# The first sweep's side work dealt at 0.6 instead of 0.56 in an attention, FFT and feed-forward kernel

## Chip, cores, metric

The kernel runs on one core of one Trainium2 chip. The metric is the device time of one execution in microseconds (us), lower is better; a time without further words is the median of several executions.

## What is computed

The inputs are q, k and v of shape (8 batches, 12 heads, 448 tokens, 64), two gains, and two weight matrices of 768 x 3072 and 3072 x 768, all fp32.

```python
q_n, k_n = rmsnorm(q, g_q), rmsnorm(k, g_k)
attn = softmax(q_n @ k_n.T / 8)
x = (attn @ v), heads side by side           # (8, 448, 768)
u = x + real(fft(fft(x, axis=1), axis=2))
un = (u - mean(u)) / sqrt(var(u) + 1e-6)     # over the last axis
out = u + relu(un @ w_ch1) @ w_ch2
```

## The kernel before, in words

Every batch goes through two kinds of work. The **side work** of a batch, `aux(b)` (L771), is attention over six pairs of heads, then three *folds* (L594, sums and differences of the attention result that only VectorE makes) and the two transforms (`spectral`, L644: `y` matmuls, `ab` matmuls, then four token tiles with the `x` transposes). The **feed-forward** of a batch, `ffn(b)` (L1035), is one *sweep* over 60 pieces of weights: 24 `up(m)` of 18 matmuls each (L1054) and 36 `down(g, d)` of 12 each (L1075), in the order up 0, then six groups of four ups (three in the last) and six downs. Each fp32 product is made from rounded high and low halves, hence three passes.

The sweep of batch b is interleaved with the side work of batch b + 1. Both are Python generators that yield a planned cost at each step: an up 3420, a down 2280; in the side work 420 for each transposed half of q or k, 760 for each of four rows of a pair's softmax, 420 + 6 x 1180 + 760 for the values of a pair of batch 1, 2000, 2000 and 3000 for its three folds, 1080 for each of four `y` steps, 980 for each of two `ab` steps and 620 for each of four token tiles. `merge` (L1106) takes a piece of the feed-forward, then side steps until the side's cost has reached the feed-forward's cost times a ratio. The ratio is `RATIO_FIRST` for batch 0 (L1160) and `RATIO` = 0.49 for the others.

Ahead of the first sweep, batch 0's side work runs alone, with 22 steps of batch 1's (`AHEAD`, L45) mixed in: these carry batch 1 through the values of its first pair. What the first sweep is given is the rest: pairs 1 to 5, folds, transforms.

The first sweep also converts weights. `bits_of` (L784) loads fp64 weights into one of two wide buffers (`dbl`) and makes fp32 of them on ScalarE (L798, L799), VectorE (L800, L804, L808) and GpSimd (L812); `convert` (L815) splits the value into high and low halves (L817 on ScalarE, L818 on VectorE). Of the 60 pieces 14 are converted before (`convert_some`, L908): downs 2 and 3 of groups 0 to 4 and ups 3, 7, 11 and 15. A piece is taken from a stream of three buffers, two streams by turns, so a piece's successor by six is refilled when it is taken. Later sweeps load converted pieces.

The order in which each engine works is not the order of the Python calls alone: the program is laid out ahead of the run by a planner (`schedule_with_timeline_sim`, L1180), which takes instructions in the order of the calls as far as its own estimate has them ready, and puts later ones ahead of those that it thinks are waiting. On the chip each engine then follows that fixed order. Result tiles of `ffn` take turns in two banks; ScalarE's relu `hs` (L1061) and VectorE's `hs` (L1062) or `acc` (L1091) free them.

Of the kernel before, what the change touches and what calls it, by code (L numbers as in the profile page):

```python
# [37 lines left out]


RATIO = 0.49  # L40
RATIO_FIRST = 0.56
CONVERT_EARLY = 0.12
EARLY = 2
DFT_STEP = 40
# [48 lines left out]
def spectral_block(ctx, tc, q, k, v, g_q, g_k, w1, w2, d1, d2, out, nb=B):  # L93
# [677 lines left out]
    def aux(b):  # L771

        EO, uns[b] = [], {}
        yield from attention(b, EO)
        yield from spectral(b, xTs[b], EO, uns[b])
# [371 lines left out]
    def behind_first():  # L1147

        fences.update(turned)
        for n, x in enumerate(second):  # L1150
            fences.clear()
            yield x
            if n < SIDE_BEHIND:
                fences.update(turned)

    for b in range(nb):
        merge(
            ffn(b, ffn_input(b, uns.pop(b)) if b else first),
            behind_first() if b == 0 else aux(b + 1) if b + 1 < nb else iter(()),
            RATIO if b else RATIO_FIRST,  # L1160
        )
# [24 lines left out]
```

## Time and profile before

| | us |
|---|---|
| median of 3 runs | 2147.34 (2145.43 to 2149.45) |
| profiled execution, its own time | 2143.77 |
| its span, first to last instruction | 2142.0 |
| first up of the first sweep starts at | 182.8 |
| first up of the second sweep starts at | 458.1 |

The profile is of one execution. TensorE (PE) is busy 97% of the span, VectorE (DVE) 72%, ScalarE (ACT) 48%, GpSimd (POOL) 16%. These shares mean little for the first 460 us, which differ from the rest; the rows below are therefore taken stretch by stretch. Times in the rows are counted from the first instruction.

### The profile page before, as it was taken

The numbers are of one execution on the slowest core, as the hardware profiler recorded it, in microseconds if no ns is written. First come the engines' busy times: TensorE is split into PE (matmuls) and PEld (weight loads), VectorE is DVE, ScalarE is ACT, GpSimd is POOL, SyncE is SP. The second block draws the span as 40 slices with busy tenths as digits, with TensorE's granted clock in tenths as the row PEclk, the third lists the DMA queues.
The fourth block names the chain that finished last, engine by engine and source line by source line (L and its number), as shares of the span: only waits on it lengthen the run. The fifth ranks groups of instructions, "written<-read, shape, count | busy, mean of one in ns | idle before, by whom it ended". The sixth has DMA issues, their size and how long they took to land.

```text
span 2142.0 us, 31168 instructions
## 1 busy us (share of the span) xinstructions
PE 2074.2 (97%) x11256; PEld 1846.0 (86%) x11256; DVE 1550.9 (72%) x2948; ACT 1024.4 (48%) x2182; POOL 342.5 (16%) x182
## 2 busy tenths in 40 slices
PE   7877999899999999999999999999999999999998
PEld 4555878799999999999999999999999989999998
DVE  6888889977885878757886778858787578764122
ACT  6857875456542555345552465425553455422100
POOL 3324334311110111001110111101010011000000
PEclk8988999999999999999999999999999999999999
DMA  6538867776556855657555755667556674458774
GB/s 186 183 122 287 267 230 239 265 243 194 175 166 197 236 169 170 188 184 225 162 176 176 237 182 173 180 188 233 168 174 186 193 210 138 152 174 250 236 251 150
DMA packets 283550, 423.86 MB, mean 198 GB/s; under 512 B 181075, under 2 KB 200516, under 8 KB 283396
## 3 DMA queue, kind: packets, MB, share of 16 engines
q1 hardware_dynamic: 278962, 419.75, 63.6%
q10 hardware_dynamic: 4434, 2.11, 0.4%
q8 instruction: 90, 1.47, 0.3%
q14 instruction: 64, 0.52, 0.1%
HBM read 362.01 MB, written 65.31 MB: 199 GB/s over the span
## 4 chain that ended last, share of the span: by engine, by line
PE 84%; DVE 5%; DMA 4%; ACT 4%; POOL 1%; issue 1%; SPq 0%; DVEq 0%; ACTq 0%; POOLq 0%
PE o L1075 30%; PE h L1054 29%; PE S L416 6%; PE av L529 4%; PE pt L517 4%; DMA dbl<-w 2%; PE y L660 2%; PE qk L352 1%; PE av L491 1%; ACT P L117 1%; PE S L411 1%; PE oT L1011 1%; PE x L691 1%; PE un L923 1%; POOL mag L812 1%
## 5 line engine op out<-in xcount | busy, mean ns | idle before, releaser
L1075 PE MATMUL o<-hs,w 128*128 128x448 f32 x3456 | 787.0, 371 | 6.2 <-ACT hs L117 2.5
L1054 PE MATMUL h<-unT,w 128*128 128x448 f32 x3456 | 788.6, 370 | 0.4 <-ACT unT L117 0.4
L1075 PEld LDWEIGHTS o<-hs,w 128*128 128x128 f32 x3456 | 636.4, 188 | 61.1 <-ACT hs L117 2.8
L1054 PEld LDWEIGHTS h<-unT,w 128*128 128x128 f32 x3456 | 637.5, 188 | 53.8 <-issue 1.9
L117 ACT ACTIVATE P<-S,mn 112x448 f32<-112x448 f32 x384 | 244.1, 638 | 231.4 <-DVE mn L117 227.0
L117 DVE TENSOR_REDUCE mn<-S 112x1 f32<-112x448 f32 x384 | 233.2, 617 | 45.0 <-PE S L416 36.3
L117 ACT ACTIVATE hs<-h 128x448 fp32r<-128x448 f32 x192 | 104.4, 544 | 297.0 <-PE h L1054 296.2
L117 DVE TENSOR_TENSOR acc<-o,acc 128x448 f32<-128x448 f32 (+1 forms) x240 | 147.0, 615 | 122.4 <-PE o L1075 121.0
L117 DVE SCALAR_TENSOR_TENSOR hs<-h,hs 128x448 fp32r<-128x448 f32 x192 | 119.1, 620 | 138.8 <-ACT hs L117 137.6
L117 POOL TENSOR_TENSOR qkn<-raw 112x1024 f32<-112x1024 f32 x36 | 68.2, 1894 | 687.4 <-PE qk L352 590.1
L117 POOL TENSOR_TENSOR ss<-ss,nhalf 112x16 f32<-112x16 f32 x48 | 144.0, 3001 | 200.4 <-DVE ss L117 172.9
L117 ACT CAST T<-pt 128x448 fp32r<-128x448 f32 x216 | 113.5, 532 | 108.4 <-PE pt L517 105.9
L529 PE MATMUL av<-T,vhl 128*128 128x448 f32 x432 | 151.7, 383 | 0.0
L117 DVE TENSOR_TENSOR T<-pt,T 128x448 fp32r<-128x448 f32 x216 | 131.6, 616 | 25.8 <-ACT T L117 24.7
L416 PE MATMUL S<-KD,QT 128*112 128x448 f32 x328 | 126.7, 386 | 4.8 <-ACT P L117 4.4
L117 DVE TENSOR_SCALAR P<-P,sm 112x448 f32<-112x448 f32 x288 | 126.8, 479 | 4.0 <-DMA values<-v 0.3
L517 PE MATMUL pt<-ident,P 112*128 112x112 f32 x864 | 125.2, 259 | 0.0
L416 PE MATMUL S<-rounded,QT 128*112 128x448 f32 x328 | 120.3, 367 | 0.1
L517 PEld LDWEIGHTS pt<-ident,P 112*128 112x128 f32 x864 | 103.7, 140 | 16.3 <-DVE R L117 0.3
L812 POOL TENSOR_TENSOR mag<-mag,dbl 128x768 uint32<-128x768 uint32 (+1 forms) x33 | 77.4, 2347 | 153.9 <-DVE mag L808 99.1
L117 POOL TENSOR_TENSOR rstd<-st,nhalf 112x1 f32<-112x1 f32 (+2 forms) x32 | 19.2, 600 | 494.0 <-DVE st L117 487.9
L529 PEld LDWEIGHTS av<-T,vhl 128*128 128x128 f32 x432 | 80.8, 188 | 8.3
(120 smaller groups left out, 2502.0 us busy)
## 6 DMA issues: line engine op xcount, KB each, us to landing
w<-w SPq DMA_DIRECT2D x192, 768.0 KB, 4.8
w<-w SPq DMA_DIRECT2D x288, 512.0 KB, 4.2
dbl<-w SPq DMA_DIRECT2D x20, 768.0 KB, 5.4
dbl<-w SPq DMA_DIRECT2D x13, 1024.0 KB, 5.6
raw<-q SPq DMA_DIRECT2D x96, 112.0 KB, 3.4
raw<-k SPq DMA_DIRECT2D x96, 112.0 KB, 3.9
values<-v SPq DMA_DIRECT2D x96, 96.0 KB, 4.4
u_dram<-u SPq DMA_DIRECT2D x24, 336.0 KB, 7.5
```

What stands on the lines that cost most here:

```text
L117: ins = emit(*args, **kwargs)
L352: nc.tensor.transpose(pt[:, c * C : (c + 1) * C], qk[:, i, c].rearrange("t h d -> t (h d)"), ident[:C, :C],)
L411: nc.tensor.matmul(s_, QT[hs, x, cs], KD[hs, z], start=step == 0, stop=step == 2)
L416: ins = nc.tensor.matmul(s_, QT[:, h, cs], K[:, h], start=step == 0, stop=step == 1)
L491: nc.tensor.matmul(av[:, :S], vhl[:, 3 * h + j].rearrange("s h d -> s (h d)"), T, start=h + j == 0, stop=False,)
L517: nc.tensor.transpose(pt[:, c * C : (c + 1) * C], Pc[c][:, 512 * h + j * 128 : 512 * h + (j + 1) * 128], ident[:C, :C],)
L529: nc.tensor.matmul(av[:, :S], lv, T[:, i], start=(j == 0 and i == 0), stop=False)
L660: nc.tensor.matmul(o, src[:, par, t0 : t0 + n], D1[:, ri, par, cols], start=i != 1, stop=i != 0,)
L691: nc.tensor.transpose(xp[:n, i * 128 : (i + 1) * 128], src[:, 3 * half + i], ident)
L812: behind(nc.gpsimd.tensor_tensor(out=bits, in0=bits, in1=low, op=ALU.add))
L1054: pace(nc.tensor.matmul(o, w[:, a, c], unT[c][:, z], start=n == 0, stop=n == 17))
L1075: pace(nc.tensor.matmul(o, w[:, a, f], hs[4 * g + f][:, z], start=n == 0, stop=n == 11))
```

## The change

One constant is different. Nothing is added or removed from what any engine does; the places of the side steps between the pieces of the first sweep are what the constant sets.

```diff
 RATIO = 0.49
-RATIO_FIRST = 0.56
+RATIO_FIRST = 0.6
 CONVERT_EARLY = 0.12
```

## Rows read from the trace of the kernel before

**Rows 1.** Busy time in stretches: us, each engine's busy us (instructions), clock, DMA share, GB/s.
```profile
core 0: us, PE busy (x) PEld busy (x) DVE busy (x) ACT busy (x) POOL busy (x), PEclk, DMA share, GB/s
183.00:320.00 137.00, 132.00 (x664) 110.79 (x665) 113.90 (x170) 104.58 (x199) 49.05 (x26) 0.98 0.77 255
320.00:380.00 60.00, 58.32 (x296) 48.65 (x295) 56.44 (x77) 34.47 (x65) 28.28 (x11) 1.00 0.70 233
380.00:420.00 40.00, 34.55 (x179) 30.49 (x178) 38.41 (x49) 19.10 (x30) 12.44 (x6) 0.91 0.77 266
420.00:458.00 38.00, 38.00 (x210) 35.01 (x210) 32.05 (x67) 20.92 (x40) 7.46 (x6) 1.00 0.77 267
458.00:707.00 249.00, 248.81 (x1389) 227.71 (x1388) 186.37 (x376) 115.83 (x256) 30.95 (x16) 1.00 0.63 190
```
**Rows 2.** Timeline of PE around 400 us: start, length, what, idle time before and releaser.
```profile
400.02 0.47 PE L1075 MATMUL o<-hs,w 128*128 128x448 f32 x1 [2.46 <-ACT hs L117]
401.58 1.11 PE L1075 MATMUL o<-hs,w 128*128 128x448 f32 x2 [1.10 <-DVE hs L117]
404.59 3.61 PE L660 MATMUL y<-D,eo 128*113 128x130 f32 x16 [1.89 <-DVE eo L117]
```
**Rows 3.** Timeline of ACT in the same stretch.
```profile
393.33 0.19 ACT L117 COPY xT<-xT 128x1 f32<-128x1 f32 x1 [4.51 <-DVE xT L117]
395.26 0.89 ACT L798 ACTIVATE mag<-dbl 128x768 f32<-128x768 f32 x1 [1.75 <-DMA dbl<-w]
...
398.63 0.90 ACT L798 ACTIVATE mag<-dbl 128x768 f32<-128x768 f32 x1 [1.66 <-DMA dbl<-w]
399.44 0.52 ACT L117 ACTIVATE hs<-h 128x448 fp32r<-128x448 f32 x1
```
**Rows 4.** Timeline of DVE (last fold, conversions) and of POOL in the same stretch.
```profile
384.50 0.68 DVE L818 TENSOR_TENSOR w<-mag,w 128x512 fp32r<-128x512 f32 x1
...
388.56 2.67 DVE L804 TENSOR_SCALAR mag<-mag 128x768 uint32<-128x768 uint32 x1
...
393.74 1.52 DVE L117 TENSOR_TENSOR eo<-xT 128x449 f32<-128x449 f32 x2
...
397.74 0.55 DVE L804 TENSOR_SCALAR mag<-mag 128x768 uint32<-128x768 uint32 x1
...
405.46 1.08 DVE L117 TENSOR_TENSOR tot<-tot,eo 128x900 f32<-128x900 f32 x1
...
388.29 2.52 POOL L812 TENSOR_TENSOR mag<-mag,dbl 128x1024 uint32<-128x1024 uint32 x1 [6.79 <-DMA values<-v]
```
**Rows 5.** Timeline of PE: last value matmul of batch 1's pairs 1, 2, 3 and 5.
```profile
255.47 0.91 PE L498 MATMUL av<-R,values 128*128 128x448 f32 x2
281.70 0.92 PE L498 MATMUL av<-R,values 128*128 128x448 f32 x2
316.41 0.91 PE L498 MATMUL av<-R,values 128*128 128x448 f32 x2
...
383.43 0.91 PE L498 MATMUL av<-R,values 128*128 128x448 f32 x2
```
**Rows 6.** Timeline of PE: one whole up and one whole down.
```profile
426.46 3.84 PE L1054 MATMUL h<-unT,w 128*128 128x448 f32 x18
...
445.36 2.69 PE L1075 MATMUL o<-hs,w 128*128 128x448 f32 x12
```
**Rows 7.** Busy time in three stretches of the early sweep, columns as in rows 1.
```profile
200.00:220.00 20.00, 17.00 (x82) 14.46 (x81) 16.29 (x25) 14.20 (x27) 5.66 (x4) 0.91 0.82 251
220.00:260.00 40.00, 38.62 (x198) 32.58 (x197) 35.32 (x52) 32.20 (x63) 18.69 (x8) 1.00 0.89 288
280.00:320.00 40.00, 39.57 (x200) 32.05 (x199) 30.73 (x50) 29.48 (x58) 13.36 (x9) 1.00 0.75 250
```
**Rows 8.** Waits of PE in 183 to 458 us: total, times, longest; then one DVE group there.
```profile
PE S L416 <- ACT P L117: 4.4, 4, 2.0
...
L818 DVE TENSOR_TENSOR w<-mag,w 128x512 fp32r<-128x512 f32 x26 | 26.5, 1018 | 0.4 <-ACT w L817 0.4
```

## The prediction

> **What bounds the kernel now.** I read the busy times by stretch first [rows 1]. From 458 us on the kernel is TensorE alone: 248.81 of 249 us busy at full clock. An edit that only re-places side steps of the first sweep can gain nothing there, and can lose only if it makes that flow wait. In the first sweep PE is idle for 5.0 us of 183 to 320, 1.7 of 320 to 380, 5.45 of 380 to 420, and not at all after. The granted clock says the rest: 0.91 over 380 to 420 means 18% of 40 us at the lower of the two levels, 7.2 us in which half the work is done, so 3.6 us lost; likewise 0.98 of 137 us is 2.7 us. So the sweep holds 12.2 us of idle time and 6.3 us of clock, 18.5 in all, and 9.0 of them (5.45 + 3.6) stand in one place, 380 to 420. That is all that a better deal could win, and the largest single prize in it is 9.0.
>
> Next what PE waits for in that place [rows 2]: 2.46 us for ScalarE's `hs`, 1.10 for VectorE's `hs`, 1.89 for the `eo` of the last fold, which the first `y` matmul needs. Together 5.45, the whole idle time of the stretch. Why `hs` is late is seen on ACT [rows 3]: it stands in ACT's order behind a copy that waited 4.51 us for VectorE and two conversion steps that waited 1.75 and 1.66 us for weights. VectorE is what stands behind this: 56.44 of 60 us busy in 320 to 380, 38.41 of 40 in 380 to 420 [rows 1], while in 280 to 320 it had 9.3 of 40 us free [rows 7]. The last fold took from 393.74 to 406.5 on VectorE [rows 4], with steps of conversions between its own, as the one at 397.74. So the reading is: VectorE is overfull in the last half of the sweep's side work and has room just before.
>
> **What the change moves.** It removes and adds no instruction and no wait of its own, so every cost is one of place. The planned costs say where. The side work left is 4620 (eleven halves of q or k at 420) + 15200 (five pairs' softmax) + 41300 (five pairs' values at 8260) + 7000 (folds) + 8760 (transforms) = 76,880; the sweep is 24 x 3420 + 36 x 2280 = 164,160. At 0.56 the last side step is dealt when the sweep has reached 76,880 / 0.56 = 137,286, which is behind down(4,4) at 137,940; at 0.6 at 128,133, behind down(4,0) at 128,820. The end of the side work moves four downs forward. Counting the same way: the last value step of pairs 1 to 5 moves from down(0,4), down(1,1), up 12, up 14, up 17 to down(0,3), down(1,0), up 11, up 13, down(3,3); the folds from up 15, down(3,3), up 18 to up 13, down(3,0), down(3,4); the `y` steps from up 19 and 20 and down(4,0) to ups 17 and 18. In time, a piece is 3.84 us for an up and 2.69 for a down [rows 6]. The last fold passes down(3,5), up 17 and up 18: 2.69 + 3.84 + 3.84 = 10.4 us of feed-forward that now comes behind it. The tail passes four downs, 10.8 us.
>
> Does the chip follow the deal? The last value matmul of a pair tells its place [rows 5]. Against the deal at 0.56 pair 1 comes five pieces late (dealt at down(0,4), run just ahead of down(1,0)), pair 2 three late, pair 3 two, and pair 5 on its place, at the end of up 17. From pair 1 to 2 it took 26.2 us, from 2 to 3 34.7, and 67.0 for the two pairs behind. So early on the side work is held by its own chain (it ran a pair in 26.2 us when it was behind), and the ratio hardly matters; from pair 3 on it has caught up and the deal holds it back. There 0.6 acts: I take pair 5 to end some 7 to 9 us sooner, with the three pieces that it passes run later.
>
> **The sum.** Work taken off 320 to 400 has to fit before: 280 to 320 has 9.3 us of VectorE free [rows 7], so the moved steps find room there. Whatever passes behind the folds takes its conversions along, so fewer of them stand between the fold's operations. The `y` wait (1.89) is the one that the change reaches directly; the clock loss (3.6) follows the idle time. The two `hs` waits (3.56 together) come from ACT's order behind conversions and may stay. Bounds: from below 9.0 (all of it goes), from above 0 (the same queues form one group sooner) or a loss (a second such place). I take 1.89 + 3.6 = 5.5 us gained, because the hs waits alone, 3.56 in two pieces, lie near those of 1.7 us in 60 that left the clock at 1.00 in 320 to 380 [rows 1]; they are also not far from the 3.0 of 200 to 220, with clock 0.91 [rows 7], so the gain is not safe. At the end of the sweep nothing is gained: 420 to 458 has no idle time to win, and what follows is as full [rows 1].
>
> The profiled execution took 2143.77 us, 1.77 around its span of 2142.0; the median is 3.57 above it. I put the difference on the median: 2147.34 - 5.5 = 2141.8 (2138.3 by the profiled execution).
>
> **The rivals.** *The queues move along* (0.30). VectorE is overfull from 320 on whatever the order. If the fold is merely overfull sooner, the stall of 9.0 us stands one group earlier at the same price: 2147, give or take 3. For it: the lag of rows 5, and that the planner's order, not the deal alone, sets the place. Against it: the 9.3 us free in 280 to 320. The change not doing what it says is this case too: side steps that are not ready don't come sooner for being dealt sooner.
>
> *The tail runs short of weights* (0.04). With no side work beside downs (4,1) to (5,5), the pieces follow each other faster by these 10.8 us, while twelve of the fourteen are converted within the sweep. The refill looks six pieces ahead, some 16 to 23 us of feed-forward by rows 6, against one conversion's chain of ACT, VectorE and GpSimd, so I expect only that part of the gain is given back: 2146.
>
> *Slower: ACT fills up early* (0.16). Place: 200 to 260 us. ACT is busy 32.2 of 40 us in 220 to 260, and PE already waits 4.4 us in four pieces for `P` of the softmax [rows 7, 8]. The new deal is up to two steps ahead in the first ups (five instead of three behind up 0, level again behind up 2, two ahead behind up 4). A softmax row has two exponentials of 448 columns, and a relu of that size took 0.52 us [rows 3], so I estimate 1 to 2 us of ACT a step, up to 4 us against 7.8 + 5.8 us free in 220 to 260 and 200 to 220. If they stand in ACT's order ahead of `hs`, PE gets a second place like 200 to 220, which costs 3.0 us idle and 1.8 of clock, 4.8 in all, while the late stall stays: 2152. It decides once the pulled work passes ACT's free 13.6 us or stands ahead of a late weight load; the first is unlikely by these numbers, the second can't be seen in this trace.
>
> *Slower: VectorE is held by GpSimd* (0.09). The 388.56 instruction of VectorE took 2.67 us while GpSimd's add of 388.29 ran for 2.52; the same kind took 0.55 at 397.74 [rows 4]. The 26 splits of 512 columns took 1.018 us on average [rows 8] against 0.68 for the one at 384.50: 8.8 us lost in the sweep. VectorE has 3.6 us free in 320 to 380 and 1.6 in 380 to 420. If the denser deal makes two more meetings of 2.1 us there, 4.2 us pass through to PE, with nothing gained: 2151.5. The Trainium skill, "SBUF — State Buffer", section "Who interferes with whom", has a rule behind this: VectorE and GpSimd share a pair of ports that one holds for a whole instruction while the other blocks, and who comes first decides. By that rule the price per meeting is the rest of GpSimd's instruction, and packing side work denser next to conversions speaks against the change; the trace agrees on the size of one meeting.
>
> **How the numbers follow.** Forecast 0.41 (2138 to 2143); queues move along 0.30; tail 0.04; ACT 0.16; GpSimd 0.09. A measurement of this kernel tells some 0.2%, 4.3 us, from no change. Faster by more: 0.41. Slower by more: most of the two slower cases, 0.25. Within: 0.34. For the range, the lower end lets all 9.0 go and 2 us of the early idle time with it: 2136. The upper end takes the ACT case with 2 us on top: 2154. Cases of both signs are in it; the forecast's own range is 2138 to 2143.
>
> **What would show it.** If right: in 280 to 320 VectorE is busier than 30.7 of 40 us; pair 5's last value matmul comes by about 376; the first `y` matmul comes ahead of 398 with no wait for `eo`; 380 to 420 has clock 1.00 and under 4 us idle; the next sweep begins at about 452.6 instead of 458.1, and everything behind is the same but shifted. If the queues move along: the same waits for `hs` and `eo` stand one group sooner and the second sweep begins within 2 us of 458. If ACT fills up: PE's wait for `P` passes 7 us in 200 to 260. If GpSimd holds VectorE: the splits' mean is above 1.02 us. I would be wrong altogether if the difference lay behind the second sweep's start, where I expect none.

## The result, and the profile after

| | before | after |
|---|---|---|
| median of 6 runs each, us | 2146.64 | 2157.28 |
| lowest to highest | 2143.75 to 2149.45 | 2155.78 to 2160.61 |
| profiled execution, its own time | 2143.77 | 2156.59 |
| first up of the first sweep at | 182.8 | 186.5 |
| length of the first sweep | 275.3 | 287.1 |
| length of the second sweep | 248.7 | 245.1 |

The change made the kernel slower: 1.0053 times the time of before, 95% interval 1.0040 to 1.0066. The prediction was 2141.8 us with a range of 2136 to 2154: wrong in sign, and outside the range.

The two profiled executions stand 12.8 us apart, 2 more than the medians, so differences between the traces are read with that margin. Up to the first sweep each engine has the same instructions in the same order in both, so the 3.7 us there (182.8 against 186.5) say nothing of the change, and stretches of after are taken 3.7 us later than those of before. The first sweep is 11.8 us longer, the second 3.6 shorter; 23 matmuls have moved from the second to the first (18 of batch 2's side work, five transposes of the first batch's output).

Busy time by stretch of after; the columns are those of [rows 1], and the stretches are those of [rows 1] moved by 3.7 us. The second fence has the same view of after and of before over their first two sweeps.

```profile
186.70:323.70 137.00, 131.60 (x667) 110.42 (x668) 117.17 (x177) 107.37 (x207) 54.71 (x26) 0.98 0.76 251
323.70:383.70 60.00, 53.99 (x253) 44.06 (x252) 50.41 (x66) 30.62 (x55) 24.29 (x10) 0.94 0.63 209
383.70:423.70 40.00, 36.98 (x207) 33.85 (x206) 35.54 (x49) 17.56 (x28) 13.55 (x5) 1.00 0.75 246
423.70:461.70 38.00, 33.49 (x183) 29.35 (x182) 34.05 (x67) 25.21 (x46) 10.27 (x7) 1.00 0.75 270
```
```profile
186.50:473.60 287.10, 268.11 (x1370) 228.70 (x1370) 247.99 (x379) 187.06 (x347) 104.92 (x49) 0.98 0.73 245
473.60:718.70 245.10, 245.10 (x1364) 224.51 (x1363) 177.74 (x356) 109.27 (x240) 29.27 (x15) 1.00 0.62 190
...
182.80:458.10 275.30, 263.15 (x1345) 225.23 (x1346) 241.09 (x360) 179.37 (x332) 97.42 (x48) 0.98 0.76 254
458.10:706.90 248.80, 248.61 (x1388) 227.51 (x1387) 186.17 (x375) 115.63 (x256) 30.95 (x16) 1.00 0.63 190
```

PE's idle time, stretch by stretch: 5.4 us (before 5.0), 6.0 (1.7), 3.0 (5.45), 4.5 (none). The stall that the prediction wanted to remove did shrink, by 2.4 us, and its clock went from 0.91 to 1.00. Two new ones outweigh it: 4.3 us more from 324 to 384, with the clock at 0.94 there (12% of 60 us at the lower level, 3.6 us lost, just what the late stretch lost before), and 4.5 at the end of the sweep. Together 6.8 us more idle time and no less clock lost. The moved matmuls add about the 3.6 us that the second sweep gave up; some 1.4 us of the sweep's 11.8 are left without a name.

What PE waits for in the two new places, and for `y` (timeline of PE, after; columns as in [rows 2]):

```profile
348.85 3.94 PE L1054 MATMUL h<-unT,w 128*128 128x448 f32 x18 [0.74 <-DVE acc L117]
355.71 5.07 PE L1054 MATMUL h<-unT,w 128*128 128x448 f32 x16 [2.72 <-DVE hs L117]
374.77 1.02 PE L491 MATMUL av<-T,values 128*128 128x448 f32 x2 [2.55 <-ACT T L117]
401.65 2.15 PE L660 MATMUL y<-D,eo 128*113 128x130 f32 x16 [2.34 <-DVE eo L117]
427.62 2.72 PE L1075 MATMUL o<-hs,w 128*128 128x448 f32 x12 [1.25 <-DVE acc L117]
435.94 2.71 PE L1075 MATMUL o<-hs,w 128*128 128x448 f32 x12 [2.74 <-DVE acc L117]
```

The first: an up's result bank is free only when VectorE has made the second half of `hs`. Timeline of VectorE, then GpSimd and ScalarE, after:

```profile
351.93 1.21 DVE L117 TENSOR_REDUCE ss<-qkn 112x16 f32<-112x1024 f32 x1
353.06 2.07 DVE L800 TENSOR_SCALAR mag<-mag 128x768 f32<-128x768 f32 x1
355.05 0.61 DVE L117 SCALAR_TENSOR_TENSOR hs<-h,hs 128x448 fp32r<-128x448 f32 x1
...
362.42 2.95 DVE L117 TENSOR_TENSOR qkn<-raw,ss 112x512 f32<-112x512 f32 x2 [2.26 <-POOL ss L117]
...
351.47 3.23 POOL L812 TENSOR_TENSOR mag<-mag,dbl 128x768 uint32<-128x768 uint32 x1 [6.78 <-ACT mag L798]
357.37 5.01 POOL L117 TENSOR_TENSOR ss<-ss,nhalf 112x16 f32<-112x16 f32 x1 [2.67 <-DVE ss L117]
...
351.31 0.53 ACT L117 ACTIVATE hs<-h 128x448 fp32r<-128x448 f32 x1
...
373.17 1.14 ACT L799 ACTIVATE dbl<-dbl 128x1024 uint32<-128x1024 uint32 x1 [6.42 <-DMA dbl<-w]
```

ScalarE's half is done at 351.84, VectorE's starts only at 355.05. In between stand a sum of squares (`ss`, 1.21 us) and a conversion step that took 2.07 us where 0.55 is its time alone. The sum is not in this sweep's deal: it is the q/k norm of batch 2's second pair, work of the *second* sweep's side, which the planner has laid forward. It had done so in before too, only the place differs: 175.4 us behind the first up there, 165.4 here. In before the sum stood between two `hs` steps that nothing waited for (timeline of VectorE, before):

```profile
356.53 0.57 DVE L117 SCALAR_TENSOR_TENSOR hs<-h,hs 128x448 fp32r<-128x448 f32 x1
...
358.21 1.20 DVE L117 TENSOR_REDUCE ss<-qkn 112x16 f32<-112x1024 f32 x1
...
362.17 0.61 DVE L117 SCALAR_TENSOR_TENSOR hs<-h,hs 128x448 fp32r<-128x448 f32 x1
```

The second, 2.55 us for `T`, starts on the SP queue. Timeline of SP, after and then before:

```profile
355.21 0.49 SPq L866 DMA_DIRECT2D w<-w  x1
365.40 0.33 SPq L239 DMA_DIRECT2D raw<-q  x1
365.83 0.43 SPq L795 DMA_DIRECT2D dbl<-w  x1
...
351.49 0.38 SPq L795 DMA_DIRECT2D dbl<-w  x1
...
365.83 0.87 SPq L239 DMA_DIRECT2D raw<-q  x2
```

After, SP stands from 355.7 to 365.4 at the q load of batch 2's next pair, whose buffer the norm's multiplies (362.42) still read. A weight load waits behind it until 365.83; before, the same weight load stood ahead and went at 351.49. ScalarE then waits 6.42 us for the weights (373.17), with `T` behind it in its order, and PE waits for `T` at 374.77.

The third is the pair of waits for `acc` at the end of the sweep. Ahead of the longer one, 2.74 us, VectorE's order has another conversion step that met an add of GpSimd: it took 2.74 us, where 0.69 is its time alone. Timeline of VectorE and GpSimd, after:

```profile
429.08 2.74 DVE L800 TENSOR_SCALAR mag<-mag 128x1024 f32<-128x1024 f32 x1
...
428.83 2.45 POOL L812 TENSOR_TENSOR mag<-mag,dbl 128x1024 uint32<-128x1024 uint32 x1 [8.44 <-ACT mag L798]
```

The shorter wait, 1.25 us, was not traced to a single step.

### The profile page after: what moved, and what is told of

It reads as the page before. It is cut to its first block, busy times and chain, and to the rows that moved or that the text cites. A ratio compares the mean times of both kernels' runs of the same rounds, so it can differ in the third digit from the quotient of the medians.

```text
span 2154.8 us, 31170 instructions
## 1 busy us (share of the span) xinstructions
PE 2078.6 (96%) x11256; PEld 1847.4 (86%) x11256; DVE 1548.9 (72%) x2948; ACT 1024.6 (48%) x2182; POOL 347.8 (16%) x182
## 3 DMA queue, kind: packets, MB, share of 16 engines
q10 hardware_dynamic: 4434, 2.11, 0.4%
## 4 chain that ended last, share of the span: by engine, by line
PE 79%; DVE 7%; DMA 6%; ACT 4%; issue 2%; POOL 1%; SPq 1%; DVEq 0%; ACTq 0%; POOLq 0%
PE o L1075 29%; PE h L1054 27%; PE S L416 5%; PE av L529 4%; PE pt L517 4%; DMA dbl<-w 4%; PE y L660 1%; PE qk L352 1%; PE av L491 1%; DMA ur<-u_dram 1%; ACT P L117 1%; DVE mn L117 1%; DVE w L818 1%; PE oT L1011 1%; PE x L691 1%
## 5 line engine op out<-in xcount | busy, mean ns | idle before, releaser
L491 PE MATMUL av<-T,values 128*128 128x448 f32 x144 | 74.6, 608 | 17.1 <-ACT T L117 15.8
```

The costliest lines, as they stand in the source:

```text
L491: nc.tensor.matmul(av[:, :S], vhl[:, 3 * h + j].rearrange("s h d -> s (h d)"), T, start=h + j == 0, stop=False,)
```

## The experiments

Every kernel here computes all of the reference; only the order of work differs, and in two of them the stage in which weights are converted. Where an experiment *holds* an instruction, it calls `follow` (L148) on it: that ties it, in the planner's order only, behind the last feed-forward matmul issued ahead of its call, with no wait added on the chip. Ratios are to the kernel before on the same chip, with 95% intervals.

| kernel | ratio | interval | median, before's |
|---|---|---|---|
| 0.6 as changed | 1.0053 | 1.0040 to 1.0066 | 2157.28, 2146.64 |
| hold06 | 1.0035 | 1.0024 to 1.0045 | 2155.89, 2147.59 |
| early06 | 1.0047 | 1.0030 to 1.0064 | 2157.61, 2147.59 |
| late06 | 1.0002 | 0.9993 to 1.0011 | 2148.72, 2147.59 |
| r058 | 1.0010 | 1.0001 to 1.0018 | 2150.11, 2147.59 |
| hold2_06 | 1.0000 | 0.9992 to 1.0009 | 2147.30, 2146.90 |
| hold2_056 | 0.9992 | 0.9983 to 1.0000 | 2145.33, 2146.90 |
| pre056 | 1.0717 | 1.0702 to 1.0732 | 2300.48, 2146.90 |
| pre06 | 1.0716 | 1.0702 to 1.0731 | 2300.30, 2146.90 |
| holdnorm_06 | 1.0004 | 0.9994 to 1.0013 | 2147.65, 2146.45 |
| holdmult_06 | 1.0046 | 1.0034 to 1.0059 | 2156.19, 2146.45 |
| hold2_early06 | 1.0053 | 1.0041 to 1.0066 | 2157.56, 2146.45 |
| hold2_058 | 1.0040 | 1.0026 to 1.0054 | 2153.72, 2146.45 |
| holdsum_06 | 1.0005 | 0.9996 to 1.0014 | 2148.40, 2147.75 |
| r057 | 1.0005 | 0.9996 to 1.0014 | 2148.17, 2147.75 |
| r059 | 1.0018 | 1.0009 to 1.0026 | 2151.28, 2147.75 |
| r062 | 1.0056 | 1.0043 to 1.0069 | 2161.78, 2147.75 |
| r053 | 1.0024 | 1.0016 to 1.0033 | 2153.48, 2148.05 |
| hold2_053 | 1.0036 | 1.0025 to 1.0046 | 2155.34, 2148.05 |

**Is it the load on SP?** hold06 is 0.6 with batch 2's q/k loads held.

```diff
-                nc.sync.dma_start(
+                ins = nc.sync.dma_start(
                     raw[:, i, h],
                     src[b, 2 * p + h].rearrange("(c t) d -> t c d", c=NC),
                 )
+                if b == 2 and p > 1:
+                    follow(ins)
```

> Ratio 0.6, and the loads of batch 2's q and k from its third pair on (L239) may not be laid ahead of the second sweep's matmuls, so that no weight load of the first sweep stands behind them on SP. Theory A (a load of q and k, which waits for its buffer, holds up the weight load behind it on SP, ACT then waits for weights and TensorE for ACT): the wait of about 10 us of the load of group 4's downs 0 and 1 goes, ACT's wait of 6.4 us for it too, TensorE's wait for T near 374 us falls from 2.6 us to under 0.5, and 3 to 6 of the 10.6 us lost come back: 2151 to 2154. Theory B (side steps stand ahead of hs and acc in VectorE's order, and with two result banks TensorE waits for them): the waits for hs and acc (6.8 us) stay, and the time stays at 2155 to 2158. Theory C (any new order of the planner draws another set of stalls, worth several us either way): no relation, anywhere from 2145 to 2160.

It gave back about a third, 1.0035; the two intervals overlap a little, so the size is rough. By time, the run lies in theory B's range. PE's waits in 320 to 385 us of it (total, times, longest):

```profile
PE h L1056 <- DVE hs L117: 2.7, 1, 2.7
PE h L1056 <- DVE acc L117: 0.7, 1, 0.7
PE av L493 <- ACT T L117: 0.4, 1, 0.4
```

The wait for `T` falls from 2.5 us to 0.4, so the chain from the SP queue to it is shown; the `hs` wait stays, as do 4.0 us for `acc` later. The load is a part, not the cause of the whole. (The conversion step ahead of the longer `acc` wait took 2.73 us here too.)

**Which half of the deal costs?** early06 deals at 0.6 to 52% of the sweep and lets 0.56 catch up; late06 the other way round. r058 is the value between.

```diff
-            while side_done < done * ratio:
+            while side_done < ratio(done):
...
-            RATIO if b else RATIO_FIRST,
+            (lambda d: d * RATIO) if b else (lambda d: max(0.56 * d, 0.6 * min(d, 85500))),   # early06
+            (lambda d: d * RATIO) if b else (lambda d: 0.56 * d if d < 85500 else 0.6 * d),   # late06
```

> Ratio 0.6 up to the end of group 2 of the first sweep (planned cost 85,500), then no more side steps until 0.56 has caught up, and 0.56 behind that. Theory B (denser side work near the folds is what VectorE can't take, so the loss belongs to the second half): about 2147 to 2149. Theory A (the q and k loads of batch 2 come early because the side work of the first half is early): 2151 to 2155. Theory C: anywhere from 2145 to 2160.

> Ratio 0.56 up to the end of group 2 of the first sweep (planned cost 85,500), then 0.6, which takes some five side steps at once at that point. Theory B (the second half holds the loss): 2154 to 2158, as with 0.6 throughout. Theory A: between, 2148 to 2153. Theory C: anywhere from 2145 to 2160.

> Ratio 0.58, half of the change. Theories A and B, in which the loss grows with the density: 2149 to 2154, between 2146.6 and 2157.3. Theory C (the order decides, and a small change of the ratio draws a new one): not in between, or as far off as 0.6 is.

The early half alone costs as much as the whole (1.0047), the late half nothing (1.0002). That speaks against theory B. The value between, 0.58, lies between (1.0010), as theories A and B said. In early06 PE does not wait behind the sum of squares, but behind the norm's two multiplies, and behind the load on SP at a higher price. Its timelines of SP, ScalarE, VectorE and PE:

```profile
368.23 0.33 SPq L239 DMA_DIRECT2D raw<-q  x1
368.66 0.43 SPq L795 DMA_DIRECT2D dbl<-w  x1
...
375.64 1.10 ACT L799 ACTIVATE dbl<-dbl 128x1024 uint32<-128x1024 uint32 x1 [10.40 <-DMA dbl<-w]
...
365.27 2.93 DVE L117 TENSOR_TENSOR qkn<-raw,ss 112x512 f32<-112x512 f32 x2 [2.26 <-POOL ss L117]
368.12 0.61 DVE L117 SCALAR_TENSOR_TENSOR hs<-h,hs 128x448 fp32r<-128x448 f32 x1
...
368.79 0.67 PE L1075 MATMUL o<-hs,w 128*128 128x448 f32 x2 [2.11 <-DVE hs L117]
378.00 1.86 PE L491 MATMUL av<-T,values 128*128 128x448 f32 x2 [5.71 <-ACT T L117]
```

The same weight load stands behind the same q load; ScalarE waits 10.40 us and PE 5.71. The same norm stands ahead of an `hs`, at another of its steps: VectorE waits 2.26 us for the power, multiplies for 2.93, and PE waits 2.11. Both mechanisms are seen in both deals, with other shares.

**Is it batch 2's norm, pulled into the first sweep?** hold2_06 holds the loads and also the squares with which batch 2's norm begins (GpSimd makes them from batch 2 on); holdnorm_06 holds the squares alone. hold2_056 does what hold2_06 does at 0.56.

```diff
-            G.tensor_tensor(out=sq, in0=flat, in1=flat, op=ALU.mult)
+            ins = G.tensor_tensor(out=sq, in0=flat, in1=flat, op=ALU.mult)
+            if b == 2 and p > 0:
+                follow(ins)
```

> As the run with the loads of q and k held back at 0.6, and in addition the norm of batch 2's pairs from the second on (first step: the squares on GpSimd) may not be laid ahead of the second sweep's matmuls. That takes one pair's norm off the first sweep: 2 us of squares and 3 to 5 us of power on GpSimd, some 4 us on VectorE. Theory A (loads on SP): no better than 2155.9, since the loads are held already. Theory B (VectorE overfull between 320 and 400 us): TensorE's waits for hs and acc fall from 6.8 us to under 4, 2149 to 2153. Theory C (each order draws its own stalls): no relation, 2145 to 2160.

> The same two holds at 0.56. Theory A: nothing to win at 0.56, 2146 to 2149. Theory B: the late stall of 9.0 us at 380 to 420 shrinks too, 2140 to 2145. Theory C: no relation, 2143 to 2158; a loss here would show that a new order of the planner alone costs as much as the change did.

> 0.6 with the norm alone held (squares of batch 2's pairs from the second on not ahead of the second sweep's matmuls); the loads of q and k are free again, so the load for the third pair may stand in SP's order in the first sweep. Theory D (the second pair's norm, which the planner lays into the first sweep, is what costs at 0.6, not the loads): 2146 to 2150, like the 2147.3 with both held. Theory A (the loads on SP carry the loss): 2152 to 2156.

Held, the loss is gone: 1.0000, and 1.0004 with the squares alone (which also delays the q load, since its buffer comes free behind the norm). The norm of batch 2's second pair now runs about 280 us after the sweep's first up instead of 165, and with it the `hs` wait at 356 is gone; of the other late waits that for `y` falls from 2.34 us to 0.70 and the longest for `acc` from 2.74 to 0.84 (in holdnorm_06, where the conversion step at 424 us took 0.69). At 0.56 there is little to gain: 0.9992, with an interval that ends at no change. No run of this study clearly beats the kernel before.

**Which instruction of the norm?** After the squares come VectorE's sum, GpSimd's power and VectorE's two multiplies. holdsum_06 holds the sum, holdmult_06 the multiplies, each with the rest left free.

```diff
-        V.tensor_reduce(ss, sq, axis=AX.X, op=ALU.add)
+        ins = V.tensor_reduce(ss, sq, axis=AX.X, op=ALU.add)      # holdsum_06
+        if b == 2 and p > 0:
+            follow(ins)
...
-            V.tensor_tensor(
+            ins = V.tensor_tensor(                                 # holdmult_06
                 out=qk[:, i].rearrange("t c h d -> t h c d"),
...
+            if b == 2 and p > 0:
+                follow(ins)
```

> 0.6 with VectorE's sum of the squares of batch 2's pairs from the second on held out of the first sweep, and with it the power and the multiplies; the squares on GpSimd stay. If sum and power carry the price (the sum and a blocked step of 2.07 us stand ahead of hs on VectorE at 352 to 355 us): 2146 to 2150. If the squares on GpSimd do: 2153 to 2158.

> 0.6 with only the last step of that norm held: VectorE's two multiplies (L282, 2.95 us, in the changed kernel 2.26 us of VectorE waiting at their head for GpSimd's power), while the squares, VectorE's sum and GpSimd's power stay in the first sweep. The loads that need the buffer behind the multiplies move too. Theory D1 (the wait at the head of VectorE's order, with relu's second half queued behind it, is the price): 2146 to 2150. Theory D2 (the work of the norm on GpSimd and VectorE and their blocking of each other is the price): most of the loss stays, 2153 to 2157.

Holding the multiplies changes nothing that can be told from 0.6 (1.0046); holding the sum, and with it the power, recovers nearly all (1.0005). Timelines of VectorE and PE in holdmult_06, then VectorE's and PE's waits from 320 to 385 us in holdsum_06:

```profile
353.16 1.20 DVE L117 TENSOR_REDUCE ss<-qkn 112x16 f32<-112x1024 f32 x1
354.29 2.06 DVE L802 TENSOR_SCALAR mag<-mag 128x768 f32<-128x768 f32 x1
356.28 0.61 DVE L117 SCALAR_TENSOR_TENSOR hs<-h,hs 128x448 fp32r<-128x448 f32 x1
...
356.94 3.53 PE L1056 MATMUL h<-unT,w 128*128 128x448 f32 x16 [2.73 <-DVE hs L117]
```
```profile
355.49 0.55 DVE L802 TENSOR_SCALAR mag<-mag 128x768 f32<-128x768 f32 x1
355.96 0.61 DVE L117 SCALAR_TENSOR_TENSOR hs<-h,hs 128x448 fp32r<-128x448 f32 x1
...
427.22 0.69 DVE L802 TENSOR_SCALAR mag<-mag 128x1024 f32<-128x1024 f32 x1 [0.79 <-ACT mag L800]
...
PE av L493 <- ACT T L117: 1.4, 1, 1.4
PE h L1056 <- DVE acc L117: 0.7, 1, 0.7
```

The conversion and `hs` follow each other in both; with the sum out of the way the conversion takes 0.55 us, and PE has no `hs` wait. The later `acc` waits go as well, from 4.0 us in after (3.8 in holdmult_06) to 1.2. There the step at 427.22 meets no add and takes 0.69 us; in after, hold06 and holdmult_06 it meets one and takes 2.73 or 2.74, and the longest `acc` wait is 2.6 to 2.7 us. So the longer `acc` wait goes with that meeting. That holding the sum undoes the meeting is shown; why is not, since a held step changes the planner's order of all that follows.

**Does it need the conversions?** pre056 and pre06 convert the other 40 pieces of weights ahead of the sweep too, which puts its first up some 170 us later, and leave only loads of converted pieces in it.

```diff
+    for p in PIECES[6:]:
+        if p not in early:
+            name = "e" + "_".join(str(x) for x in p)
+            streams[stream_of(0, p)].converted(p, name)
+            early.add(p)
```

> Ratio 0.56, with all weights that the first sweep would convert converted ahead of it (46 less the first six pieces), so that the sweep loads finished pieces and VectorE, ACT and GpSimd have the side work, relu and sums alone. The stage ahead of the sweep grows by far more than the sweep wins: 2250 to 2350 in all. What counts is the sweep's own length, 275.3 us before: about 250 to 262 by every theory.

> The same with 0.6. Theories A and B (the loss needs the conversions beside the side work): the same time as with 0.56 within 2 us. Theory C (a new order of the planner draws new stalls, whatever else runs): a difference of 4 us or more either way.

First sweep, 0.56 and then 0.6 (busy time, columns as in [rows 1]):

```profile
352.30:613.90 261.60, 257.59 (x1336) 223.82 (x1337) 131.92 (x239) 108.12 (x235) 27.56 (x18) 0.99 0.60 189
352.70:615.40 262.70, 259.17 (x1343) 225.07 (x1344) 137.33 (x246) 111.88 (x244) 31.63 (x20) 0.98 0.59 187
```

The medians are 0.2 us apart. With no conversions beside it, the step from 0.56 to 0.6 has no price that can be told. These rows also tell what conversions cost the sweep: 275.3 - 261.6 = 13.7 us at 0.56, and 24.4 at 0.6.

**Is the norm the price of every deal?** The same hold on other deals, and other ratios without it (`RATIO_FIRST` = 0.53, 0.57, 0.59, 0.62).

> 0.6 up to the end of group 2 and held behind it until 0.56 has caught up, which alone took 2157.6, with norm and loads of batch 2 held as in the run that took 2147.3 at 0.6. Theory D (the norm is what costs): 2146 to 2150. If the early density costs by itself: 2154 to 2158.

> Both holds at 0.58, between 2145.3 at 0.56 and 2147.3 at 0.6. Theory D: the ratio hardly matters once the norm is out, 2144 to 2148. Theory C (each order draws its own stalls): 2142 to 2156.

> Ratio 0.57. If the loss grows with the density: 2147 to 2149, between 2147 at 0.56 and 2150.1 at 0.58. If each deal draws its own order and stalls: 2144 to 2157, and with 0.59 and 0.62 not on one rising line.

> Ratio 0.59. If the loss grows with the density: 2152 to 2155, between 2150.1 at 0.58 and 2157.3 at 0.6. If each deal draws its own stalls: 2145 to 2160.

> Ratio 0.62. If the loss grows with the density: 2160 or more. If each deal draws its own stalls: 2145 to 2160, as likely under 2157 as over.

> Ratio 0.53; the last side step is dealt behind down(5,0) or so, 145,057 of 164,160. If the density alone sets the time: 2140 to 2145, some 1 us less per 0.01 as from 0.59 to 0.56. If 0.56 stands at a floor: 2145 to 2149. If the side work then ends too late for the second sweep: 2150 or more.

> 0.53 with norm and loads of batch 2's later pairs held out of the first sweep. If the hold is worth 1.7 us as at 0.56: 1 to 3 us under the run at 0.53 without it. If the gain at 0.56 was its order's luck: no relation to that run.

It is not. The hold gains nothing in sum for early06 (1.0053 against 1.0047), as was expected if the early density costs by itself: it shortens the first sweep, 287.6 to 281.6 us, and the second and third are 5.4 and 1.4 us longer. At 0.58 it makes things worse (1.0040 against 1.0010), and if anything at 0.53 too (1.0036 against 1.0024), against the gain that was expected of it. With the hold at 0.58 PE waits 5.0 us for the `eo` of the last fold, and the third sweep is 3.1 us longer. At 0.62 the largest wait is again for `hs`, elsewhere:

```profile
408.54 5.86 PE L1054 MATMUL h<-unT,w 128*128 128x448 f32 x16 [7.06 <-DVE hs L117]
```

There a fold step and the conversions stand ahead of `hs` on VectorE. At 0.59 the norm's sum stands earlier still, 161.5 us behind the first up (165.4 at 0.6), and the loss is only 0.18%. Without a hold, the ratio to before runs 1.0024 (0.53), 1 (0.56), 1.0005, 1.0010, 1.0018 (0.59), 1.0053 (0.60), 1.0056 (0.62): 0.56 is a low place with a rise on both sides and, in these medians, a jump between 0.59 and 0.60.

The rise above 0.56 is also what was expected of a loss that grows with the density: 0.57, 0.58 and 0.62 lie in the ranges given for it, 0.59 less than 1 us below. In the profiled executions, one of each kernel, the first sweep, from its first up to the next sweep's, grows at every step, from 275.3 us (0.56) through 279.3, 282.1, 284.7 and 287.1 (0.60) to 291.5 (0.62); the first two sweeps together take 524.0, 526.8, 530.4, 532.6, 532.2 and 539.2, with no jump at 0.60. Against a price of density alone stand 0.53, which should have been faster then and took 2153.48 (its two sweeps 532.0), and hold2_06, which needs 524.4 at 0.6.

**What follows.** Each ratio gives another order to all engines. At 0.6 three of PE's new waits are traced. Ahead of the `hs` wait (2.72 us) stand the sum of a later batch's norm and a conversion that meets an add of GpSimd; ahead of the `T` wait (2.55 us), a q load before a weight load on SP; ahead of the longer `acc` wait (2.74 us), another such meeting. Holding the load took the second away and gave back about a third; holding the sum took the first away, shortened the second to 1.4 us and the third to 0.9, and gave back nearly all, at the same ratio. So at 0.6 the time depends on the order and not on the ratio alone. How much each single step costs is not shown, because a hold changes all that follows it, and on other deals the same hold gained nothing or cost time. That denser dealing also has a price of its own is neither shown nor excluded: the ratios without a hold fit it above 0.56. Open, too, are the losses of the other deals, which were not taken apart wait by wait; the 1.4 us in the first sweep's matmuls; and why the held orders make the second or third sweep longer than before's at some ratios and not at 0.6.

## Why the prediction was wrong

- **The place of the gain: right.** The first `y` matmul came 6.7 us sooner in the sweep, 215.1 us behind the first up instead of 221.8 [rows 2], against 10.4 us of pieces that the last fold was to pass. 380 to 420 lost 2.4 us of its idle time and 3.6 of its clock loss, 6.0 against a forecast of 5.5. But the named wait was the wrong one: `eo` still holds `y` up, for 2.34 us, before 1.89 [rows 2], and it is the `hs` waits, said to stay, that went from that stretch. That the two sums lie so near is luck.
- **"The moved steps find room there": the step that failed.** From 280 to 320 VectorE went from 30.73 us [rows 7] to 31.96, so little of the free 9.3 us was used, 1.2 us. The last value matmul of batch 1's fifth pair came at 383.38, or 379.7 with the 3.7 us taken off, against a forecast of 376; before it came at 383.43 [rows 5], so it moved by 3.7 us and not by 7 to 9. The work met folds, conversions and batch 2's norm between 340 and 365 instead.

```profile
383.38 0.92 PE L498 MATMUL av<-R,values 128*128 128x448 f32 x2
...
280.00:320.00 40.00, 37.98 (x192) 30.52 (x191) 31.96 (x50) 29.79 (x61) 16.08 (x9) 1.00 0.72 234
```

- **"VectorE is overfull": right for the place, and not enough.** In 340 to 360, where `hs` is late, VectorE was busy 19.68 of 20 us, before 18.00, and PE lost 3.5. But in holdnorm_06 VectorE is as full there, 19.67, and PE loses nothing. What was short was not VectorE's time alone but the place of single steps in its order; a share of busy time could not tell the two apart, the steps ahead of the late `hs` could. (VectorE's busy time over the whole stretch of 60 us *fell*, from 56.44 [rows 1] to 50.41. That comes behind the stall: it stood 2.26 us for GpSimd's power and 6.83 us for a conversion whose weights were late.) The stretch in after, then in holdnorm_06:

```profile
340.00:360.00 20.00, 16.53 (x73) 13.89 (x72) 19.68 (x31) 11.87 (x23) 8.90 (x4) 0.91 0.68 227
340.00:360.00 20.00, 20.00 (x107) 17.40 (x106) 19.67 (x29) 12.00 (x24) 7.92 (x4) 1.00 0.78 262
```

- **"Every cost is one of place": true, and too narrow.** Place was taken as the place of this sweep's side steps. The planner also lays steps of the batch after next into this sweep and sets them among the critical ones. The norm of batch 2's second pair stood there before too and came 10 us earlier; 23 matmuls and a third set of squares came over from the second sweep. No term of the sum stood for that, and neither the bound "a second such place" nor its 9 us was carried into the forecast's range.
- **No difference behind the second sweep's start: nearly right.** The second sweep is 3.6 us shorter, from the same moved matmuls; the later ones differ by about 1 us in all.
- **The rivals.** *Queues move along* had the best of it: a stall did form one group sooner, with the clock loss of the old one, but part of the old one stayed and another came at the end of the sweep, which it did not have. *ACT fills up early* is refuted: the softmax matmuls' wait for `P` fell from 4.4 us [rows 8] to 0.5, and 1.0 us of other matmuls' waits for it came up. *VectorE held by GpSimd* was right on the kind of meeting and wrong in its sign: the splits' mean, which was to rise above 1.02 us, fell to 0.900. But two meetings stood ahead of PE's waits, 1.5 us at 353.06 ahead of `hs` and 2.05 at 429.08 ahead of `acc`, 3.6 us in all against the 4.2 that the case had. *The tail short of weights* was not seen: PE's new waits at the end of the sweep are for `acc`, not for weights.

```profile
L818 DVE TENSOR_TENSOR w<-mag,w 128x512 fp32r<-128x512 f32 x26 | 23.4, 900 | 0.9 <-ACT w L817 0.8
```

The range ended at 2154 because it took one rival at a time: a gain in one place and a loss in two others was not among the cases.

## What to carry to other kernels

Where a planner turns calls into fixed orders, a pacing constant need not have a smooth price: each value draws a new order, and the profile must be read for which step stands ahead of the one that frees a matmul's bank, or ahead of a load that an engine needs next. Look for steps of later batches there first, and hold the one step; holding the sum of squares recovered nearly all that 0.6 had lost, and a like hold made 0.58 worse, so it has to be tried on the very order it is for. An engine's busy share does not tell whether its order hurts: VectorE was as full with the stall as without it.

## What was unexpected of the hardware

**A conversion step waits out GpSimd's add.** The conversion step of 0.55 us took 2.07 beside GpSimd's add and ended at 355.13, 0.43 us behind that add's end at 354.70; the step of 0.69 us took 2.74 at 429.08 and ended 0.54 us behind the add beside it. The sum of squares took 1.21 us beside the first of these adds, as it did with GpSimd idle (1.20). The Trainium skill, "SBUF — State Buffer", section "Who interferes with whom", says that the two engines share a pair of ports which one of them holds for a whole instruction, that a scalar step can ask for that pair, and that a reduction on this chip never does: these rows agree with all three. GpSimd's instructions grew too: the add at 351.47 took 3.23 us and the next of its kind 1.87, the power at 357.37 took 5.01 and the one in before 2.90. Which of VectorE's steps did that, the rows do not tell.

**The clock does not follow the length of a wait alone.** After the waits of 2.72 and 2.55 us in 324 to 384 the granted clock of that stretch fell to 0.94, a part of it at 1.2 GHz, and 16 matmuls took 5.07 us where 18 took 3.94 just before. The wait of 2.74 us at 435.94 left its stretch at 1.00, with 12 matmuls in 2.71, and in holdmult_06 the 16 matmuls behind the same `hs` wait, 2.73 us, took 3.53. So a PE wait of this size cost its own length or some 1.5 us more, and which of the two was not told by the wait.
